# A batch-2 attention decode step with an MLP beside it: the linear layers turned round, the last transfers cut and ordered anew

## The chip, the core and the metric

The kernel runs on one core of a Trainium2 chip. A core has a matrix engine (TensorE, PE in the profile; its weight loads are PEld), a vector engine (DVE), a scalar engine (ACT), GpSimd (POOL), a sequencer that here only issues transfers (SP), and 16 DMA engines between HBM and the on-chip memory SBUF. TensorE writes to PSUM, which has banks of 512 fp32 values in each of 128 partitions. The metric is the time of one execution on the device in microseconds, a median over runs.

## The reference

With x of 2 rows by 1024 (batch 2, one token), cut to what matters:

```python
q = x @ wq                                   # 2 x 4096: 32 heads of 128
scores = einsum(q, k_cache) * Dh ** -0.5     # k_cache, v_cache: 2 x 32 x 16384 x 128, bf16
a = einsum(softmax(scores), v_cache).reshape(2, 1, 4096) @ wo
h = gelu(layernorm(x) @ w1)                  # then a shift along the sequence
x1 = x + shifted(h) @ w2
b = x1 + gelu(layernorm(x1) @ w3) @ w4       # w3: 1024 x 3584, w4: 3584 x 1024
return g * a + (1 - g) * b                   # g = sigmoid of (x * gate_w).sum()
```

With one token the shift leaves zeros. The two caches are 537 MB, the weights some 35 MB.

## The kernel before

**Units.** The attention is cut into NU = 32 units u, each a pair of heads (hp = u // 2) for one of the two batch rows b = u % 2. A unit has 8.4 MB of K and 8.4 MB of V, each loaded by one DMA of 128 partitions x 64 KB. Row s of the cache lies so that a partition holds 256 consecutive rows j.

**Memory.** One tile `mem` has five cells of 32 KB per partition. K of even units lies in cells 0 and 1, of odd units in cells 1 and 2; so two consecutive K loads share cell 1. V lies in cells 3 and 4 (V of unit 30 in cells 0 and 1). At the start wq lies in cells 3 and 4, w1 and w2 in cell 2; w3 follows in cells 3 and 4, and w4 after it in the same place.

**Main loop.** For n from 0 to 31: `score_first(n)` (K chunks transposed by DVE at L424, multiplied by PE at L430, first the half that shares a cell with the next K); `load_k(n+1)`; `score_second(n)`; the softmax in two steps, `softmax_a(n)` and `softmax_b(n)`; in between, for n of 2 and more, `pv(n-2)` (L502: probabilities as stationary operand, V streamed in 512 columns, into four column groups of the PSUM bank `oacc`), `load_v(n-1)`, and `pv_end(n-2)` (L515 copies the bank, four fp32 matmuls at L520 with the constant `sel8` add the four groups and transpose, L532 scales into `OT`). When both batch rows of a head pair are done, `wo_project(hp)` (L403) adds that pair's share of the output into two PSUM banks `arow`. Every fourth n, `load_wo` loads wo for four heads, 1 MB, into a single buffer.

**The linear layers.** q (L249) and the four layers of the MLP (L219, class `LinearT`) use the weight matrix as stationary operand in blocks of 128 x 128 and stream the two activation columns past it; the result comes out transposed, as the next step needs it. lin1, lin2 and lin3 run at n = 0, lin4 at n = 1. lin3's `load` stands behind q, lin4's behind lin3 and V of unit 0 behind lin4, since each takes the place of the one before.

**The end.** For n = 31, V of unit 30 is loaded first and V of unit 31 in nine pieces (`PIECES`, counted in rows j: seven of 32, two of 16; 32 rows are 1 MB). `pv_last` streams the first six pieces as in `pv`, and takes the rest with V as stationary operand (L547), one matmul for each j. Then L554 scales, `wo_project(15)` adds the last pair, DVE and ACT copy one output bank each, and SP stores both in one DMA. The last `load_wo` (n = 29, heads 28 to 31) is cut by partitions into five DMAs: `cuts = (0, 1, 3, 7, 16, P)`.

**What sets the order.** All DMAs are issued by SP in program order; each waits in SP's queue until its destination is free, and what stands behind it waits too. The framework derives the waits from the tiles' regions, and uses eight DMA semaphores in turn. Of one DMA, each of the 16 engines moves a fixed share of the partitions, and it takes its shares of successive DMAs one after another.

Of the kernel before, what the change touches and what calls it, by code (L numbers as in the profile page):

```python
# [23 lines left out]
def kernel(  # L24
# [15 lines left out]
    nc = tc.nc  # L40
# [35 lines left out]
    def misc_psum(shape, dtype=FP32):  # L76
        return mps.tile(shape, dtype, tag="misc", name="misc")
# [116 lines left out]
    for k in range(NP):  # L194
        t = const.tile([P, NJ // 4, 2, 4], BF16, name=f"pt{k}")
        nc.gpsimd.memset(t[:], 0.0)
        pts.append(t)

    class LinearT:

        def __init__(self, W, actT, name, cell, offset):
# [9 lines left out]
        def load(self):  # L211
            nc.sync.dma_start(out=self.dst, in_=self.src)

        def compute(self):
            wc = self.dst.rearrange("p (r n) -> p r n", n=self.N)
            ps = misc_psum([P, self.C, B])
            for c in range(self.C):
                for r in range(self.R):
                    nc.tensor.matmul(  # L219
                        ps[:, c, :],  # L220
                        lhsT=wc[:, r, :].rearrange("p (m c) -> p c m", c=self.C)[:, c, :],
                        rhs=self.actT[:, r, :],
                        start=(r == 0),
                        stop=(r == self.R - 1),
                    )
            nc.vector.tensor_copy(out=self.acc[:], in_=ps[:])

    xn1T = mlp.tile([P, KC, B], BF16)
# [15 lines left out]
    nc.vector.tensor_copy(out=xT[:], in_=xin[:].rearrange("p b r -> p r b"))  # L244

    qps = misc_psum([P, H, B])
    for h in range(H):
        for r in range(KC):
            nc.tensor.matmul(  # L249
                qps[:, h, :],  # L250
                lhsT=wq_t[:, r, h * Dh : (h + 1) * Dh],
                rhs=xT[:, r, :],
                start=(r == 0),
                stop=(r == KC - 1),
            )
    lin3.load()
    qT = const.tile([P, H, B], BF16)
# [79 lines left out]
    def gelu_T(pre, dst, C):  # L337
# [10 lines left out]
        )  # L348
        nc.vector.tensor_tensor(out=dst, in0=th[:], in1=pre, op=ALU.mult)

    def mlp_post1():
# [9 lines left out]
        layernorm_T(x1T[:], xn2T[:], "ln2")  # L361

    NH2 = D // 512
    arow = [rps.tile([B, 512], FP32, name=f"arow{k}") for k in range(NH2)]

    def mlp_post4():

        omg = mlp.tile([P, B], FP32, name="omg")
        nc.vector.tensor_scalar(
            out=omg[:], in0=g_rep[:], scalar1=-1.0, scalar2=1.0, op0=ALU.mult, op1=ALU.add  # L370
        )
        nc.vector.tensor_tensor(out=bT[:], in0=lin4.acc[:], in1=x1T[:], op=ALU.add)
        nc.vector.tensor_tensor(
            out=bT[:], in0=bT[:], in1=omg[:].unsqueeze(1).to_broadcast([P, KC, B]), op=ALU.mult
        )
        W = 512 // KC
        for k in range(NH2):
            for c in range(KC):
                nc.tensor.matmul(  # L379
                    arow[k][:].rearrange("b (m c) -> b c m", c=KC)[:, c, :],  # L380
                    lhsT=bT[:, c, :],
                    rhs=ident_f[:, k * W : (k + 1) * W],
                    start=(c == 0),
                    stop=False,
                    skip_group_check=True,
                )
# [3 lines left out]
    wo_view = A_wo.rearrange("(h d) n -> d h n", d=Dh)  # L390
    wo_tiles = {}

    def load_wo(q):
        t = wopool.tile([P, WOH, D], BF16, name="wo")
        cuts = (0, P) if q < H // WOH - 1 else (0, 1, 3, 7, 16, P)
        for a, z in zip(cuts, cuts[1:]):
            nc.sync.dma_start(out=t[a:z], in_=wo_view[a:z, q * WOH : (q + 1) * WOH, :])
        wo_tiles[q] = t

    def wo_project(hp):  # L400
        for k in range(NH2):
            for h in (2 * hp, 2 * hp + 1):
                nc.tensor.matmul(  # L403
                    arow[k][:],
                    lhsT=OT[:, h, :],
                    rhs=wo_tiles[h // WOH][:, h % WOH, k * 512 : (k + 1) * 512],
                    start=False,
                    stop=(h == H - 1),
                    skip_group_check=True,
                )  # L410

    S_tiles = {}
    st_tiles = {}
# [44 lines left out]
    def softmax_b(u):  # L458
        st, Dm = st_tiles.pop(u)
        R_ps = misc_psum([P, P])  # L460
        nc.tensor.matmul(R_ps[:], lhsT=ones_f[:], rhs=Dm[:], start=True, stop=True)  # L461
        nb = stat.tile([P, 1], FP32, name="nb")
        rs = stat.tile([P, 1], FP32, name="rs")
        Pt = pts[u % NP]
        halves = [slice(e * HALF, (e + 1) * HALF) for e in range(2)]
        for rows in halves:
            nc.vector.tensor_reduce(out=nb[rows], in_=R_ps[rows, rows], axis=AX.X, op=ALU.min)  # L467
        for e, rows in enumerate(halves):
            nc.scalar.activation(  # L469
                out=Pt[rows, :, e, :].rearrange("p (m a) k -> p a k m", a=GT // 4),  # L470
                in_=st[rows, :, 0:NG].rearrange("p (a k) m -> p a k m", k=4),
                func=ACTF.Exp,
                bias=nb[rows],
                scale=scale,
                accum_out=rs[rows],
            )
# [51 lines left out]
    def pv_end(u):  # L528
        hp, b = units[u]
        ot = misc_psum([P, 2])  # L530
        pv_sum(u, ot, True, True)
        nc.vector.tensor_scalar(  # L532
            out=OT[:, 2 * hp : 2 * hp + 2, b], in0=ot[:], scalar1=g_rep[:, b : b + 1],
            scalar2=None, op0=ALU.mult,
        )
        if b == B - 1:
            wo_project(hp)

    def pv_last(u):
        hp, b = units[u]  # L540
        ot = misc_psum([P, 2])
        moving = sum(PIECES[:6]) // 4
        pv_moving(u, 0, moving, moving)
        pv_sum(u, ot, False, False)
        V = v_view(u)
        for j in range(4 * moving, NJ):
            nc.tensor.matmul(  # L547
                ot[:],
                lhsT=V[:, j, :],
                rhs=pts[u % NP][:, j // 4, :, j % 4],  # L550
                start=False,
                stop=(j == NJ - 1),
            )
        nc.vector.tensor_tensor(  # L554
            out=OT[:, 2 * hp : 2 * hp + 2, b], in0=ot[:], in1=rinvs[u % NP][:], op=ALU.mult
        )
        wo_project(hp)

    for n in range(NU):
        score_first(n)  # L560
        if n == 0:
            compute_gate()
            layernorm_T(xT[:], xn1T[:], "ln1")
            lin1.compute()
            mlp_post1()
            lin2.compute()
            mlp_post2()
        if n + 1 < NU:
            load_k(n + 1)
        else:  # L570
            load_v(NU - 2)
        score_second(n)
        softmax_a(n)
        if n == 0:
            lin3.compute()
            gelu_T(lin3.acc[:], h2T[:], FC)
            load_wo(0)
            lin4.load()
        elif n == 1:
            lin4.compute()  # L580
# [12 lines left out]
    pv(NU - 2)  # L593
    pv_end(NU - 2)
    pv_last(NU - 1)

    out_row = mlp.tile([B, D], BF16)
    nc.vector.tensor_copy(out=out_row[:, 0:512], in_=arow[0][:])
    nc.scalar.activation(out=out_row[:, 512:1024], in_=arow[1][:], func=ACTF.Copy)
    nc.sync.dma_start(out=out.rearrange("b s d -> (b s) d"), in_=out_row[:])  # L600


# [28 lines left out]
```

## Time and profile before

| | |
|---|---|
| median of 3 runs | 1350.43 us (1346.7 to 1350.57) |
| the profiled execution | 1351.2 us, span 1349.2 |
| PE, DVE, ACT, POOL busy | 802.4, 643.0, 127.4, 15.3 us |
| read from HBM | 572.53 MB, 424 GB/s over the span |
| PE instructions of the linear layers | q 256 matmuls; lin1 and lin2 64 each, lin3 and lin4 224 each |
| the linear layers on PE | q from 22.91 to 33.2, lin3 from 75.26 for 14.30, lin4 from 115.95 for 13.57 us |

The page cuts the span into 40 equal slices of 33.7 us. A DMA line gives the busy share of the 16 engines, a GB/s line what they moved; the two differ where an engine is busy but slow. In rows of instruction groups the numbers are start and length in us, then the engine, the line of the kernel, and the tiles written and read. The chain of waits goes back from the last instruction, at each step to what released it.

### The profile page before, as it was taken

To read this page: it belongs to the slowest core of one execution; us is meant where nothing else is said; L and a number is where in the kernel's file an instruction comes from. 1 tells how busy PE (TensorE), PEld (TensorE's weight loads), DVE (VectorE), ACT (ScalarE), POOL (GpSimd) and SP (SyncE) were. 2 spreads that over 40 slices of the span, in tenths; PEclk is the share of its full clock that TensorE was granted. 3 is DMA by queue.
4 is the path that set the end of the run, shared out by engine and by line. 5 is a ranking of instruction groups with operands and counts; after the bars stand their busy time and mean duration, and the time that the engine had idled before them with its cause. 6 is when DMAs were issued, how large, how long until landed. Compare 5 with 4: busy or idle time off the path is not lost.

```text
span 1349.2 us, 12232 instructions
## 1 busy us (share of the span) xinstructions
PE 802.4 (59%) x5470; PEld 368.1 (27%) x5470; DVE 643.0 (48%) x501; ACT 127.4 (9%) x197; POOL 15.3 (1%) x54
## 2 busy tenths in 40 slices
PE   2679676554567645556664546666455666555464
PEld 2456222222222222222222222222222222222122
DVE  0444555543455554445555444555434455544250
ACT  0010100111111001111001111100111110011110
POOL 1000000000000000000000000000000000000000
PEclk9967887777888777778877778887667888777886
DMA  9999999999999999999999999999999999999996
GB/s 405 433 419 395 432 434 434 435 434 430 432 432 430 429 434 434 432 432 434 436 434 434 434 432 432 428 432 435 432 434 430 428 434 436 432 428 434 352 434 288
DMA packets 15803, 573.31 MB, mean 425 GB/s; under 512 B 1797, under 2 KB 1797, under 8 KB 6151
## 3 DMA queue, kind: packets, MB, share of 16 engines
q1 hardware_dynamic: 15751, 572.54, 99.0%
q8 instruction: 42, 0.69, 0.2%
q14 instruction: 10, 0.08, 0.0%
HBM read 572.53 MB, written 0.00 MB: 424 GB/s over the span
## 4 chain that ended last, share of the span: by engine, by line
DMA 67%; PE 17%; DVE 12%; issue 4%; ACT 0%; SPq 0%; POOL 0%; ACTq 0%; DVEq 0%
DMA mem<-in_A_k_cache_dram 65%; PE S L430 13%; DVE KT L424 12%; PE misc L219 3%; DMA mem<-in_A_v_cache_dram 2%; PE oacc L502 0%; PE arow L379 0%; ACT pt L469 0%; PE arow L403 0%; PE misc L547 0%; PE misc L520 0%; PE misc L461 0%; PE misc L480 0%; POOL ln_rstd L330 0%; DVE nb L467 0%
## 5 line engine op out<-in xcount | busy, mean ns | idle before, releaser
L430 PE MATMUL S<-KT,qw 128*128 128x512 bf16 x2048 | 553.1, 420 | 390.4 <-DVE KT L424 389.3
L424 DVE STREAM_TRANSPOSE KT<-mem 128x2048 f32<-128x2048 f32 x256 | 571.5, 2284 | 306.6 <-DMA mem<-in_A_k_cache_dram 247.6
L430 PEld LDWEIGHTS <-qw 128*128 128x128 bf16 x2048 | 220.2, 108 | 715.2 <-issue 540.6
L502 PE MATMUL oacc<-mem,pt 128*8 128x512 bf16 x2032 | 118.3, 384 | 16.0 <-DMA mem<-in_A_v_cache_dram 16.0
L455 ACT ACTIVATE Dm<-ident_s,m 128x128 f32<-128x128 f32 x32 | 12.9, 404 | 986.8 <-DVE m L453 986.8
L469 ACT ACTIVATE pt<-St,nb 64x256 bf16<-64x256 f32 x64 | 89.9, 1404 | 79.2 <-DVE nb L467 65.6
L532 DVE TENSOR_SCALAR OT<-misc,g_rep 128x2 bf16<-128x2 f32 x31 | 6.9, 222 | 144.9 <-PE misc L520 144.9
L502 PEld LDWEIGHTS <-pt 128*8 128x8 bf16 x2032 | 47.0, 87 | 83.6 <-issue 32.6
L480 PE MATMUL misc<-rs,lmat 128*128 128x1 f32 x62 | 17.7, 355 | 78.7 <-ACT pt L469 78.7
L482 DVE RECIPROCAL rinv<-misc 128x1 f32<-128x1 f32 x31 | 5.2, 169 | 102.2 <-PE misc L480 102.2
L451 DVE STREAM_TRANSPOSE St<-S 128x512 f32<-128x512 f32 x32 | 22.9, 717 | 63.8 <-PE S L430 63.8
L520 PE MATMUL misc<-sel,osb 128*128 128x2 f32 x256 | 34.5, 257 | 27.1 <-ACT osb L515 27.1
L520 PEld LDWEIGHTS misc<-sel,osb 128*128 128x128 f32 x256 | 31.8, 195 | 43.7 <-ACT osb L515 43.7
L480 PEld LDWEIGHTS misc<-rs,lmat 128*128 128x128 f32 x62 | 15.1, 302 | 91.4 <-ACT pt L469 91.2
L219 PEld LDWEIGHTS <-mem 128*128 128x128 bf16 x576 | 36.2, 169 | 1.7 <-issue 0.9
L469 ACT ACTIVATION_READ_ACCUMULATOR pt<-St,nb 64x1 f32 x64 | 30.6, 477 | 0.0
L515 ACT ACTIVATE osb<-oacc,rinv 128x512 f32<-128x512 f32 x31 | 21.4, 689 | 73.9 <-PE oacc L502 73.9
L249 PE MATMUL misc<-xT,mem 128*128 128x2 bf16 x256 | 7.1, 165 | 26.1 <-DVE xT L244 23.3
L281 POOL TENSOR_TENSOR qw<-qd,mask 128x16 bf16<-128x16 bf16 x32 | 8.4, 266 | 1165.1 <-PE S L430 1136.5
L403 PE MATMUL arow<-wo,OT 128*2 128x512 bf16 x64 | 20.1, 444 | 0.3 <-DVE OT L554 0.3
L467 DVE TENSOR_REDUCE nb<-misc 64x1 f32<-64x64 f32 x64 | 14.2, 222 | 5.0 <-PE misc L461 0.9
L461 PE MATMUL misc<-Dm,ones_f 128*128 128x128 f32 x64 | 15.6, 327 | 0.0
(83 smaller groups left out, 109.4 us busy)
## 6 DMA issues: line engine op xcount, KB each, us to landing
mem<-in_B_w_dram SPq DMA_DIRECT2D x2, 7168.0 KB, 29.1
wo<-in_A_wo_dram SPq DMA_DIRECT2D x7, 1024.0 KB, 31.8
mem<-in_A_v_cache_dram SPq DMA_DIRECT2D x7, 1024.0 KB, 30.0
mem<-in_B_w_dram SPq DMA_DIRECT2D x2, 2048.0 KB
mem<-in_A_v_cache_dram SPq DMA_DIRECT2D x2, 512.0 KB, 18.7
wo<-in_A_wo_dram SPq DMA_DIRECT2D x1, 896.0 KB, 35.9
mem<-in_A_k_cache_dram SPq DMA_DIRECT2D x32, 28.2
mem<-in_A_v_cache_dram SPq DMA_DIRECT2D x31, 33.3
```

The costliest lines, as they stand in the source:

```text
L219: nc.tensor.matmul(ps[:, c, :], lhsT=wc[:, r, :].rearrange("p (m c) -> p c m", c=self.C)[:, c, :], rhs=self.actT[:, r, :], start=(r == 0), ...
L403: nc.tensor.matmul(arow[k][:], lhsT=OT[:, h, :], rhs=wo_tiles[h // WOH][:, h % WOH, k * 512 : (k + 1) * 512], start=False, stop=(h == H - ...
L424: nc.vector.transpose(out=kt[:], in_=Kc.rearrange("p j d -> p (j d)").bitcast(FP32))
L430: nc.tensor.matmul(S, lhsT=t[:, v, NG - 1 - m : NG - 1 - m + P], rhs=ktb[:, half * GT : (half + 1) * GT, w, :, e], start=(first and n == 0 ...
L451: nc.vector.transpose(out=st[:].rearrange("p j r -> p (j r)"), in_=S[:])
L461: nc.tensor.matmul(R_ps[:], lhsT=ones_f[:], rhs=Dm[:], start=True, stop=True)
L467: nc.vector.tensor_reduce(out=nb[rows], in_=R_ps[rows, rows], axis=AX.X, op=ALU.min)
L469: nc.scalar.activation(out=Pt[rows, :, e, :].rearrange("p (m a) k -> p a k m", a=GT // 4), in_=st[rows, :, 0:NG].rearrange("p (a k) m -> p ...
L480: nc.tensor.matmul(tot_ps[:, 0:1], lhsT=lmat[:], rhs=rs[:], start=True, stop=True)
L502: nc.tensor.matmul(acc[QP * q : QP * q + 8, :], lhsT=pts[u % NP][:, g].rearrange("p h k -> p (h k)"), rhs=v_view(u)[:, 4 * g : 4 * g + 4, ...
L515: nc.scalar.activation(out=osb[:], in_=oacc[u % 2][:], func=ACTF.Copy, scale=rinvs[u % NP][:, 0:1] if scaled else 1.0,)
L520: nc.tensor.matmul(ot[:], lhsT=osb[:, k * Dh : (k + 1) * Dh], rhs=sel8[:, k : k + 5 : 4], start=(k == 0), stop=(last and k == 3),)
```

## The change

- **Linear layers.** `wide_bank` makes the activations (2 columns) the stationary operand and streams the weights in 512 columns past it. The K blocks r are dealt to four column groups of a PSUM bank (rows 0, 32, 64, 96), which `copy_bank` copies to SBUF, on ACT for even banks and on DVE for odd ones. Then one fp32 matmul for each 128 columns, with the copy as stationary operand and two columns of `sel8` as moving operand, adds the four groups and transposes. q does this for 8 banks, lin1, lin2 and lin4 for 2, lin3 for 7; lin3's copies go to cell 0 of `mem`. In the MLP layers the 128 columns of a select are taken with a stride of C (8 or 28) elements.
- **V of unit 31** comes in 11 pieces (six of 32, three of 16, two of 8 rows), and `pv_last` streams only the first three pieces; the other 160 rows j go through L547's form.
- **wo.** No load is cut by partitions any more. At n = 29 only heads 28 and 29 are loaded; heads 30 and 31 are loaded at n = 31, behind the pieces of V and behind `pv_end(29)` in the program.
- **The output banks.** `arow[1]` lies at partition 32 of its bank, `wo_project` alternates between the two banks, and each bank has its own copy and store, the second issued by ACT.
- **Small loads.** `load_probes`, at n = 29 after `pv_end(27)` and so between `load_v(28)` and `load_wo`, issues six DMAs of a few rows of `gate_w` into overlapping regions of a tile `probe` that nothing reads.

```diff
-    PIECES = [32] * 7 + [16] * 2
+    PIECES = [32] * 6 + [16] * 3 + [8] * 2
...
+    def copy_bank(j, dst, src):
+        if j % 2 == 0:
+            nc.scalar.activation(out=dst, in_=src, func=ACTF.Copy)
+        else:
+            nc.vector.tensor_copy(out=dst, in_=src)
+
+    def wide_bank(j, actT, weight, R, dst):
+
+        acc = oacc[j % 2]
+        for r in range(R):
+            q = r % Q4
+            nc.tensor.matmul(
+                acc[QP * q : QP * q + B, :],
+                lhsT=actT[:, r, :],
+                rhs=weight[:, r, :],
+                start=(r < Q4),
+                stop=(r >= R - Q4),
+            )
+        copy_bank(j, dst, acc[:])
...
-        def compute(self):
+        def compute(self, wide):
             wc = self.dst.rearrange("p (r n) -> p r n", n=self.N)
+            for j in range(self.N // 512):
+                at = slice(j * 512, (j + 1) * 512)
+                wide_bank(j, self.actT, wc[:, :, at], self.R, wide[:, at])
             ps = misc_psum([P, self.C, B])
             for c in range(self.C):
-                for r in range(self.R):
-                    nc.tensor.matmul(
-                        ps[:, c, :],
-                        lhsT=wc[:, r, :].rearrange("p (m c) -> p c m", c=self.C)[:, c, :],
-                        rhs=self.actT[:, r, :],
...
+                nc.tensor.matmul(
+                    ps[:, c, :],
+                    lhsT=wide.rearrange("p (m c) -> p c m", c=self.C)[:, c, :],
+                    rhs=sel8[:, 0:B],
...
-    for h in range(H):
-        for r in range(KC):
+    for j in range(H // HB):
+        qo = qwide[:, j % 2]
+        wide_bank(j, xT, wq_t[:, :, j * 512 : (j + 1) * 512], KC, qo)
+        for k in range(HB):
             nc.tensor.matmul(
...
-    arow = [rps.tile([B, 512], FP32, name=f"arow{k}") for k in range(NH2)]
+    arow_t = [rps.tile([QP * k + B, 512], FP32, name=f"arow{k}") for k in range(NH2)]
+    arow = [arow_t[k][QP * k : QP * k + B, :] for k in range(NH2)]
...
-    def load_wo(q):
+    def load_wo(h0, n):
         t = wopool.tile([P, WOH, D], BF16, name="wo")
-        cuts = (0, P) if q < H // WOH - 1 else (0, 1, 3, 7, 16, P)
-        for a, z in zip(cuts, cuts[1:]):
-            nc.sync.dma_start(out=t[a:z], in_=wo_view[a:z, q * WOH : (q + 1) * WOH, :])
-        wo_tiles[q] = t
+        nc.sync.dma_start(out=t[:, 0:n, :], in_=wo_view[:, h0 : h0 + n, :])
+        for k in range(n):
+            wo_tiles[h0 + k] = t[:, k, :]
...
+    probe = const.tile([17, 70], BF16, name="probe")
+
+    def load_probes():
+        for n, pitch, width in (
+            (17, 60, 20), (2, 512, 30), (4, 256, 40), (8, 128, 50), (11, 93, 60), (13, 78, 70),
+        ):
+            nc.sync.dma_start(
+                out=probe[0:n, 0:width],
+                in_=gate_w[0 : n * pitch].rearrange("(p f) -> p f", p=n)[:, 0:width],
+            )
...
-        moving = sum(PIECES[:6]) // 4
+        moving = sum(PIECES[:3]) // 4
...
+            if n == NU - 3:
+                load_probes()
+            if n == NU - 1:
+                load_wo(H - 2, 2)
         softmax_b(n)
         if n % 4 == 1 and n > 1:
-            load_wo(n // 4)
+            load_wo(n - 1, min(WOH, H - 2 - (n - 1)))
...
-    nc.sync.dma_start(out=out.rearrange("b s d -> (b s) d"), in_=out_row[:])
+    out_row = mlp.tile([QP + B, 512], BF16)
+    rows = out.rearrange("b s d -> (b s) d")
+    nc.vector.tensor_copy(out=out_row[0:B, :], in_=arow[0])
+    nc.sync.dma_start(out=rows[:, 0:512], in_=out_row[0:B, :])
+    nc.scalar.activation(out=out_row[QP : QP + B, :], in_=arow[1], func=ACTF.Copy)
+    nc.scalar.dma_start(out=rows[:, 512:1024], in_=out_row[QP : QP + B, :])
```

More of the change, by code (lines that the diff above doesn't have):

```diff
@@ L212, in load @@
             nc.sync.dma_start(out=self.dst, in_=self.src)
-        def compute(self):
+        def compute(self, wide):
             wc = self.dst.rearrange("p (r n) -> p r n", n=self.N)
+            for j in range(self.N // 512):
+                at = slice(j * 512, (j + 1) * 512)
+                wide_bank(j, self.actT, wc[:, :, at], self.R, wide[:, at])
             ps = misc_psum([P, self.C, B])
             for c in range(self.C):
-                for r in range(self.R):
-                    nc.tensor.matmul(
-                        ps[:, c, :],
-                        lhsT=wc[:, r, :].rearrange("p (m c) -> p c m", c=self.C)[:, c, :],
-                        rhs=self.actT[:, r, :],
-                        start=(r == 0),
-                        stop=(r == self.R - 1),
-                    )
+                nc.tensor.matmul(
+                    ps[:, c, :],
+                    lhsT=wide.rearrange("p (m c) -> p c m", c=self.C)[:, c, :],
+                    rhs=sel8[:, 0:B],
+                    start=True,
+                    stop=True,
+                )
             nc.vector.tensor_copy(out=self.acc[:], in_=ps[:])
@@ L246 @@
     qps = misc_psum([P, H, B])
-    for h in range(H):
-        for r in range(KC):
-            nc.tensor.matmul(
[L250 to L254, printed above, removed]
+    HB = 512 // Dh
+    qwide = mlp.tile([P, D], FP32, tag="wide", name="wide")[:].rearrange("p (t n) -> p t n", t=2)
+    for j in range(H // HB):
+        qo = qwide[:, j % 2]
+        wide_bank(j, xT, wq_t[:, :, j * 512 : (j + 1) * 512], KC, qo)
+        for k in range(HB):
+            nc.tensor.matmul(
+                qps[:, j * HB + k, :],
+                lhsT=qo[:, k * Dh : (k + 1) * Dh],
+                rhs=sel8[:, 0:B],
+                start=True,
+                stop=True,
             )
@@ L349, in gelu_T, with wide4 @@
         nc.vector.tensor_tensor(out=dst, in0=th[:], in1=pre, op=ALU.mult)
+    def wide4():
+        return mlp.tile([P, D], FP32, tag="wide", name="wide")[:]
     def mlp_post1():
@@ L379, in mlp_post4 @@
                 nc.tensor.matmul(
-                    arow[k][:].rearrange("b (m c) -> b c m", c=KC)[:, c, :],
+                    arow[k].rearrange("b (m c) -> b c m", c=KC)[:, c, :],
                     lhsT=bT[:, c, :],
@@ L391 @@
     wo_tiles = {}
-    def load_wo(q):
+    def load_wo(h0, n):
         t = wopool.tile([P, WOH, D], BF16, name="wo")
-        cuts = (0, P) if q < H // WOH - 1 else (0, 1, 3, 7, 16, P)
-        for a, z in zip(cuts, cuts[1:]):
-            nc.sync.dma_start(out=t[a:z], in_=wo_view[a:z, q * WOH : (q + 1) * WOH, :])
-        wo_tiles[q] = t
+        nc.sync.dma_start(out=t[:, 0:n, :], in_=wo_view[:, h0 : h0 + n, :])
+        for k in range(n):
+            wo_tiles[h0 + k] = t[:, k, :]
     def wo_project(hp):
-        for k in range(NH2):
-            for h in (2 * hp, 2 * hp + 1):
+        for h in (2 * hp, 2 * hp + 1):
+            for k in range(NH2):
                 nc.tensor.matmul(
-                    arow[k][:],
+                    arow[k],
                     lhsT=OT[:, h, :],
-                    rhs=wo_tiles[h // WOH][:, h % WOH, k * 512 : (k + 1) * 512],
+                    rhs=wo_tiles[h][:, k * 512 : (k + 1) * 512],
                     start=False,
@@ L410, in wo_project @@
                 )
+    probe = const.tile([17, 70], BF16, name="probe")
[6 more added lines that the diff above has]
+                in_=gate_w[0 : n * pitch].rearrange("(p f) -> p f", p=n)[:, 0:width],
+            )
     S_tiles = {}
@@ L563 @@
             layernorm_T(xT[:], xn1T[:], "ln1")
-            lin1.compute()
+            lin1.compute(wide4())
             mlp_post1()
-            lin2.compute()
+            lin2.compute(wide4())
             mlp_post2()
@@ L574 @@
         if n == 0:
-            lin3.compute()
+            lin3.compute(region(0, 2 * F).bitcast(FP32))
             gelu_T(lin3.acc[:], h2T[:], FC)
-            load_wo(0)
+            load_wo(0, WOH)
             lin4.load()
         elif n == 1:
-            lin4.compute()
+            lin4.compute(wide4())
             mlp_post4()
@@ L595 @@
     pv_last(NU - 1)
-    out_row = mlp.tile([B, D], BF16)
-    nc.vector.tensor_copy(out=out_row[:, 0:512], in_=arow[0][:])
-    nc.scalar.activation(out=out_row[:, 512:1024], in_=arow[1][:], func=ACTF.Copy)
-    nc.sync.dma_start(out=out.rearrange("b s d -> (b s) d"), in_=out_row[:])
+    out_row = mlp.tile([QP + B, 512], BF16)
[4 more added lines that the diff above has]
+    nc.scalar.dma_start(out=rows[:, 512:1024], in_=out_row[QP : QP + B, :])
 _INS = ['A_x', 'A_k_cache', 'A_v_cache', 'A_wq', 'A_wo', 'B_x', 'B_w1', 'B_w2', 'B_w3', 'B_w4', 'gate_w']
```

## The prediction

> **What bounds the kernel now.** I read the page's slices and queues first, then the chain of waits, then stretches of the span.
>
> ```profile
> DMA  9999999999999999999999999999999999999996
> GB/s 405 433 419 395 432 434 434 435 434 430 432 432 430 429 434 434 432 432 434 436 434 434 434 432 432 428 432 435 432 434 430 428 434 436 432 428 434 352 434 288
> q8 instruction: 42, 0.69, 0.2%
> DMA 67%; PE 17%; DVE 12%; issue 4%; ACT 0%; SPq 0%; POOL 0%; ACTq 0%; DVEq 0%
> ```
>
> All 16 DMA engines are busy throughout at about 434 GB/s, and 573 MB at that rate is 1321 us of the 1349.2. Computation matters only where it leaves a DMA engine without work, or after the last byte. The slices that fall short are the first ones, the fourth (395), slice 38 (352) and the last. Stretches around the two in the middle:
>
> ```profile
> 128.00:132.00 4.00, 3.15 (x38) 2.85 (x37) 0.88 (x5) 1.46 (x3) 0.00 (x0) 0.50 0.79 262
> 1232.00:1248.00 16.00, 8.05 (x29) 3.14 (x29) 10.06 (x5) 0.00 (x0) 0.00 (x0) 0.68 1.00 434
> 1248.00:1264.00 16.00, 12.12 (x101) 4.86 (x98) 8.86 (x6) 0.42 (x2) 0.00 (x0) 1.00 1.01 266
> 1264.00:1280.00 16.00, 1.87 (x12) 1.63 (x13) 0.84 (x4) 3.49 (x5) 0.00 (x0) 0.67 0.99 427
> ```
>
> The last two columns are DMA share and GB/s. At 128 the queue is dry (share 0.79): V(0) waits for w4's place, which lin4 holds. At 1248 the engines are busy (1.01) but move 266: the loss is 16 x (434-266)/434 = 6.2 us. What runs there is the last wo load, cut by rows into five DMAs (1, 2, 4, 9 and 112 partitions). The seven earlier wo loads, uncut, show nothing like it. The chain shows the price, and the tail:
>
> ```profile
> 1208.43 28.18 DMA mem<-in_A_k_cache_dram
> 1246.98 37.75 DMA mem<-in_A_k_cache_dram
> 1338.54 1.05 PE oacc L502 x8
> 1342.19 1.28 PE misc L547 x48
> 1343.50 0.60 PE misc L547 x16
> 1344.34 1.88 PE arow L403 x4
> 1346.24 0.59 ACT out_row L599
> ```
>
> Last I read the landings, which the trace records for each DMA once per DMA engine. An 8.4 MB K or V load takes each engine 19.36 us, 1 MB of wo 2.42 to 2.45. The engines drift apart: an instruction fetch (q8) sets one engine back about 1.45 us, and mostly the same nine are hit. So V(28), issued at 1222.73, should end at 1250.24 on the fastest engine (call it F) and, by 1236.61+19.36, at 1255.97 on the slowest. The slowest engine sets the end; its last piece lands at 1343.46.
>
> **The change part by part**, made against the profiled execution: span 1349.2, time 1351.2, which is 0.8 above the median of 1350.43.
>
> *Last wo load whole.* K(31) lands last at 1284.73. Undisturbed it would be 1236.61 + 19.36 (V28) + 2.42 (wo) + 19.36 = 1277.75. The cuts cost 6.98, and they go: **-7.0**.
>
> *Six probe loads (load_probes, at n=29 between V(28) and wo).* They write overlapping rows of one tile. SP waits for the landing of an earlier DMA whose bytes the next one overwrites, and for the DMA eight before (eight DMA semaphores):
>
> ```profile
> SPq L97 <- DMA mem<-in_A_k_cache_dram: 363.5, 28, 16.1
> SPq L108 <- DMA mem<-in_A_v_cache_dram: 23.9, 3, 13.0
> ```
>
> The first line is a K load waiting for the K load before it, where their regions share a cell. So each probe should wait for the one before, and behind the last stand wo and K(31) in SP's queue. The first is behind V(28) in its engine's ring. One step, issue to landing on an idle queue, is 1.24 us for the output store (1346.86 to 1348.10); V(0)'s first packet starts 0.95 after its issue, and with 0.35 to post the landing I take 1.45. Probes 1 to 3 pass on low-numbered engines, which are the fast ones (the cut pieces of 2 and 4 rows land early, bar one engine). The fourth uses eight engines and meets a slow one, so it lands at slowest + 0.2. Then probe 5 (1.45), probe 6's issue (0.1), wo's issue (0.45), first packet (0.95), half a wo (1.22): K(31) starts at slowest + 4.4, against + 1.2 without probes: **+3.2**. Below: 0 if nothing waits, and 1.7 if only the fifth probe meets a slow engine. Above: all five steps after the slowest engine, 3.2 + 3 x 1.45 = 7.6. The joint restart adds **+0.5**: V(0)'s first packets after the dry queue took 3.0 to 3.3 against 2.42. After it no engine is ahead or behind, and the fetches of the last 80 us put one of them 1.45 back, where the slowest engine now loses 0.6: **+0.85**.
> The Trainium skill, "DMA: Bandwidth & Descriptors", section "Anatomy of one DMA", fits a fixed 2.0 us per DMA, for loads issued by GpSimd. By it the step after the fourth probe would be dearer and the sum about 0.6 worse; the store's 1.24 speaks for less.
>
> *Wo of heads 30 and 31 after the V pieces.* Bytes are the same, **0** in transfer. SP issues it when the fourth piece has landed, some 10 us of queue before the end, so nothing runs dry.
>
> *The tail.* Now 1343.46 to 1349.18 is 5.72 after the last byte. In the new order the V sum is closed while wo's 1.22 us of transfer run: eight L547 (0.3), the scaling (0.25), hidden. If that cover were gone it would cost 0.6. After the last byte remain wo_project, whose two accumulators now sit in different column groups (1.88 becomes about 1.05; the 64 of L502 below show four groups overlapping), copy 0.7, store 1.24, closing 1.1, steps 0.1: 4.2. **-1.5** (0 if the groups do not overlap and ACT, which issues no DMA in this trace, needs 0.7 longer for its store than SP; -2 if PE is at full clock by then).
>
> *Linear layers.* The unit prices are three rows from n=29 and the old lin4:
>
> ```profile
> 1219.06 3.63 PE L502 MATMUL oacc<-mem,pt 128*8 128x512 bf16 x64
> 1222.80 0.69 ACT L515 ACTIVATE osb<-oacc,rinv 128x512 f32<-128x512 f32 x1 [1.87 <-PE oacc L502]
> 1223.54 1.05 PE L520 MATMUL misc<-sel,osb 128*128 128x2 f32 x8 [0.85 <-ACT osb L515]
> 115.95 13.57 PE L219 MATMUL misc<-h2T,mem 128*128 128x2 bf16 x224
> ```
>
> A 512-column matmul in a column group costs 57 ns (107 at half clock), a bank copy 0.69, an fp32 select two passes of 131 ns (232 at 1340, at clock 0.50). *q*: 64x57 + 64x131 = 12 us, at most 22 at half clock, against 10.4; K(0) lands at 43.76 and the q chain has 11 us to spare, so 0, with 1 us at risk. *lin1, lin2*: 0.9 + 2.1 against 4.0 each; K(1) needs only the wide part, 0. *lin3*: 14.3 becomes 3.2 + 1 (eight matmuls fill a bank in 0.46 and its copy takes 0.69, but ACT and DVE take turns) + 56 x 0.13 to 0.23 = 11.5 to 17; I take 15.4, nearer the slow end, as L219 runs at clock 0.50 there now. w4 can be issued after the wide part, near 81 where it was 89.58; the fast engines had run out at 90.36, 1.2 us dry, gone. *lin4*: V(0) waits for 56 wide matmuls (3.2 to 6) where it waited 13.57, so its issue moves from 129.56 to about 121, under the 126 that the queue needs; the 3.4 us dry (0 to 1.5 on engines already behind) go. Against this, K(2)'s issue (105.41, now needed by 105.4 for the fast engines and 107.6 for the slow) follows lin3's end, 1 to 3 us later. On the slowest engine I take **-2.0**, between -3.4 and +2. Fewer PE instructions mean some three fetches fewer of 42: 0, at best -1.5.
> The skill's "TensorEngine Tiling (Array Packing)", section "PSUM Bottleneck", says that tiling speeds the array but not the emptying of PSUM. By that rule alone, with one engine copying at the row's 0.69, lin3's seven banks would take an estimated 4.8 us and the sum would stay as it is, since w4's issue has more room than that.
>
> Sum: -7.0 + 3.2 + 0.5 + 0.85 - 1.5 - 2.0 = -5.95. From the median: 1350.4 - 5.95 = **1344.5**.
>
> **Rivals.**
> *Probes cost nothing* (SP does not wait for overlapping rows): 3.2 + 0.5 + 0.85 come back, 1340. The waits for K speak against it. 0.12.
> *The slowdown comes from any DMA on a few engines, not from the 112 shifted rows*: V(28) loses 3.7 to 4.2 again, and the gain is 2: 1348.5, no change. For it: V(28) itself was slow beside the small pieces. Against: probes carry some 40 to 140 bytes a row. 0.25, with a late lin3 in it.
> *Slower: lin3's strided fp32 selects.* L219 costs 62 ns a weight load where L249, unstrided, costs 27. If fp32 suffers likewise, 56 x 0.4 = 22 us put lin3's end 12 later, K(2)'s issue at 117 and every engine dry for 10: +10 + 2 - 6 = +6, 1356. It decides once a pass costs over about 0.3 us (end 8 later, gain gone). Against it: L520's contiguous fp32 load already takes 192 ns where L249's bf16 takes 104, so the stride may have nothing left to slow. 0.13.
>
> **How the numbers follow.** Forecast 0.5 (1342 to 1347), free probes 0.12, no change 0.25, slower 0.13. About 0.3%, 4 us, is what a measurement of this kernel can tell from no change. Faster takes nine tenths of the forecast and all of the free probes, 0.57; within 0.3%, 0.29; slower 0.14, with a little from the no-change case. The range cuts the far half of the slower case and the far end of the free probes: 1338.5 to 1353.
>
> **What would show it.** Right: near 1250 to 1264 no stretch that is busy at 266 GB/s; six short SP issues each ended by the landing before, and K(31) issued some 3 us after V(28)'s last landing; all engines within 2 us afterwards; V(0) issued before 126; under 4.5 us from the last landing to the end. Wrong: K(2) issued after 110, S matmuls of n=0 later than 48, lin3's selects over 0.3 us a pass, or probes issued back to back.

## The result, and the profile after

The changed kernel takes 1359.4 us (median of 4 runs, 1357.39 to 1360.63); the kernel before, run beside it, 1350.5 (1346.7 to 1351.18). The ratio is 1.007, with a 95% interval from 1.0047 to 1.0094: slower by some 9 us where 6 us less were forecast. The profiled execution of the changed kernel took 1360.63 us, its span is 1358.0.

The slices and queues of its page, in the lines that answer to those of before:

```profile
DMA  9987999999999999999999999999999999999996
GB/s 402 433 360 315 431 433 433 431 431 427 433 433 432 424 438 433 435 435 426 436 433 433 431 429 433 431 431 428 433 431 429 433 427 432 435 435 435 425 424 277
q8 instruction: 39, 0.64, 0.2%
DMA 67%; PE 17%; DVE 12%; issue 3%; ACT 0%; SPq 0%; POOL 0%; DVEq 0%; ACTq 0%
```

The 352 in slice 38 is gone (425 now). But the third and fourth slices, 68 to 136 us, fell from 419 and 395 to 360 and 315, and there the engines are not slow, they have nothing to do (8 and 7 tenths). Stretches of the changed kernel (us, busy time of PE, its weight loads, DVE, ACT and POOL, then granted clock, DMA share, GB/s):

```profile
112.00:122.00 10.00, 7.86 (x26) 2.95 (x26) 8.53 (x5) 0.00 (x0) 0.00 (x0) 0.72 0.01 6
123.00:127.00 4.00, 3.42 (x16) 1.40 (x15) 4.00 (x3) 0.00 (x0) 0.00 (x0) 1.00 0.83 344
1262.00:1278.00 16.00, 13.20 (x110) 5.83 (x107) 9.29 (x9) 1.57 (x3) 0.00 (x0) 1.00 1.00 423
1328.00:1333.00 5.00, 3.22 (x36) 1.13 (x39) 0.00 (x0) 0.00 (x0) 0.00 (x0) 0.53 0.74 290
```

From 112 to 122 hardly a packet starts (share 0.01): w4 has landed on all 16 engines by 114.6, and nothing stands behind it until K(2). At 1262, where the last wo load now passes, the full rate stands (423, it was 266). At 1328 there is a new gap. SP's issues around the first gap, in the kernel before and in the changed one (start, length):

```profile
64.69 0.33 SPq L97 DMA_DIRECT2D mem<-in_A_k_cache_dram  x1
89.58 0.33 SPq L212 DMA_DIRECT2D mem<-in_B_w_dram  x1
105.41 0.33 SPq L97 DMA_DIRECT2D mem<-in_A_k_cache_dram  x1
129.56 0.33 SPq L100 DMA_DIRECT2D mem<-in_A_v_cache_dram  x1
```
```profile
71.72 0.33 SPq L97 DMA_DIRECT2D mem<-in_A_k_cache_dram  x1
92.71 0.33 SPq L232 DMA_DIRECT2D mem<-in_B_w_dram  x1
121.69 0.33 SPq L97 DMA_DIRECT2D mem<-in_A_k_cache_dram  x1
135.50 0.33 SPq L100 DMA_DIRECT2D mem<-in_A_v_cache_dram  x1
```

These are K(1), w4, K(2) and V(0). K(2) goes out 16.3 us later. The chain of waits of the changed kernel says what stood in front of it:

```profile
46.29 1.88 PE misc L275 x8
51.86 0.72 POOL ln_rstd L356
52.78 2.23 DVE KT L464
55.06 5.84 PE S L470 x16
93.36 12.86 PE misc L241 x56
...
1307.50 20.63 DMA probe<-in_gate_w_dram
1328.15 4.24 DMA probe<-in_gate_w_dram
1340.98 12.88 DMA wo<-in_A_wo_dram
1353.90 1.06 PE arow L432 x4
1354.96 0.67 DVE out_row L643
```

q's last selects (L275), the layernorm behind them and the first K transposes are on the chain, where K(0)'s landing had been the releaser; then lin3's selects (L241). At the end the chain goes through the probes, and after the last wo landing (1353.90) only 4.1 us are left.

The 8.8 us of span, read on the slowest DMA engine from its landings (us):

| | before | after | difference |
|---|---|---|---|
| V(28) last, undisturbed (1236.61 + 19.36 before) | 1255.97 | 1270.2 | +14.2 |
| from there to K(31) last | 28.8 | 20.7 | -8.1 |
| from there to the last byte | 58.7 | 63.0 | +4.3 |
| last byte to end of span | 5.72 | 4.10 | -1.6 |

Of the second row, 1.2 is half of a wo load that now comes later, and lies in the third. So the uncut wo load gave -7, the probes cost some 3, the tail gave 1.6, and the beginning lost 14.

### The profile page after: what moved, and what is told of

It reads as the page before. It is cut to its first block, busy times and chain, and to the rows that moved or that the text cites. A ratio compares the mean times of both kernels' runs of the same rounds, so it can differ in the third digit from the quotient of the medians.

```text
span 1358.0 us, 11505 instructions
## 1 busy us (share of the span) xinstructions
PE 806.9 (59%) x5086; PEld 366.8 (27%) x5086; DVE 650.4 (48%) x511; ACT 133.5 (10%) x208; POOL 15.2 (1%) x54
## 4 chain that ended last, share of the span: by engine, by line
DMA 67%; PE 17%; DVE 12%; issue 3%; ACT 0%; SPq 0%; POOL 0%; DVEq 0%; ACTq 0%
DMA mem<-in_A_k_cache_dram 57%; PE S L470 12%; DVE KT L464 11%; DMA probe<-in_gate_w_dram 7%; PE misc L241 2%; DMA xin<-in_A_x_dram 2%; PE oacc L210 1%; PE misc L275 1%; DMA wo<-in_A_wo_dram 1%; DMA mem<-in_A_v_cache_dram 0%; PE oacc L542 0%; PE arow L409 0%; ACT pt L509 0%; ACT mem L201 0%; DVE wide L203 0%
## 5 line engine op out<-in xcount | busy, mean ns | idle before, releaser
L542 PE MATMUL oacc<-mem,pt 128*8 128x512 bf16 x2008 | 115.5, 382 | 8.6 <-DMA mem<-in_A_v_cache_dram 8.6
L560 PE MATMUL misc<-sel,osb 128*128 128x2 f32 x256 | 34.5, 257 | 26.7 <-ACT osb L555 26.7
L210 PE MATMUL oacc<-mem,xT 128*2 128x512 bf16 x64 | 9.4, 612 | 24.0 <-DVE xT L266 23.2
L507 DVE TENSOR_REDUCE nb<-misc 64x1 f32<-64x64 f32 x64 | 14.2, 222 | 5.0 <-PE misc L501 0.9
L275 PEld LDWEIGHTS misc<-sel,wide 128*128 128x128 f32 x64 | 14.2, 328 | 7.4 <-issue 4.4
L203 DVE COPY wide<-oacc 128x512 f32<-128x512 f32 x7 | 4.8, 691 | 22.9 <-PE oacc L210 22.9
```

The lines of the kernel that those rows point to most:

```text
L210: nc.tensor.matmul(acc[QP * q : QP * q + B, :], lhsT=actT[:, r, :], rhs=weight[:, r, :], start=(r < Q4), stop=(r >= R - Q4),)
L275: nc.tensor.matmul(qps[:, j * HB + k, :], lhsT=qo[:, k * Dh : (k + 1) * Dh], rhs=sel8[:, 0:B], start=True, stop=True,)
L542: nc.tensor.matmul(acc[QP * q : QP * q + 8, :], lhsT=pts[u % NP][:, g].rearrange("p h k -> p (h k)"), rhs=v_view(u)[:, 4 * g : 4 * g + 4, ...
L560: nc.tensor.matmul(ot[:], lhsT=osb[:, k * Dh : (k + 1) * Dh], rhs=sel8[:, k : k + 5 : 4], start=(k == 0), stop=(last and k == 3),)
```

## The experiments

Each ratio is to runs of the kernel before made together with the experiment's own: their median is 1350.38 us for e1 to e4, 1350.32 for e5 to e8 and 1349.91 for e9 to e12. Two theories for the 14 us: the new linear layers are slower, in q and lin1 to lin3, because of their fp32 selects; or the probes and the new end cost more than thought. Two for the -7: the 112 shifted rows of the last piece were slow, or any DMA on a few engines is.

**e1_linear_old**: the changed kernel with q and all MLP layers in their old form.

```diff
-            lin3.compute(region(0, 2 * F).bitcast(FP32))
+            lin3.compute()
... (lin1, lin2, lin4 and q's loop likewise)
```

> The changed kernel with q and all four MLP layers in the old form (weights stationary); everything else as changed. Theory A (the fp32 selects, at 0.22 to 0.23 us a pass, make q 15 us and lin3 4 us longer, K(2) is issued at 121.7 and all DMA engines run dry for 10 us): K(2) issued at 105 to 106, first landing of V(0) back from 162.2 to about 150.8, time 1359.4 - 11 = 1348, still with the 3.4 us dry before V(0). Theory B (the probes' waits in SP's queue cost the time): 1356 or more, since the probes stay.

Measured: 1344.75 us, 0.9961 of before [0.995, 0.9973]. V(0) is issued at 129.3 (129.6 before) and V(28) lands last at 1257.0, 13 us earlier than in the changed kernel and 1 later than before (undisturbed). So 13 of the 14 us lie in the linear layers, and all the rest of the change is worth -5.6, which is the sum of the table's other parts (-7 + 3 - 1.6).

**e2_q_old**: the changed kernel with q's old loop alone.

```diff
-    for j in range(H // HB):
-        wide_bank(j, xT, ...)
+    for h in range(H):
+        for r in range(KC):
```

> The changed kernel with only q in the old form. Theory A: S of n=0 starts at 46 and not at 55, everything up to K(2) moves 9 us earlier, K(2) issued near 113, dry only 1 to 2 us: 1359.4 - 9 = 1350.5. Theory B: unchanged, 1358 to 1360. If lin3 and not q is what counts: a gain of 4 at most, 1355.

Measured: 1348.67 us, 0.9985 [0.9976, 0.9993]. S of n=0 starts at 46.09 as before, K(2) is issued at 112.6: 9.1 earlier than in the changed kernel, still 7.2 later than before. So q carries about 9 us and lin1 to lin3 about 7. (The 7 is against the profiled run of before, which had the later of the two starts told at the end; e2 had the earlier one, and against e4, which had it too, K(2) is 10 later: 112.6 for 102.4.)

**e5_selects_bf16**: the changed kernel with the bank copies and the select's two columns in bf16.

```diff
+    sel8b = const.tile([P, 8], BF16)
+    nc.vector.tensor_copy(out=sel8b[:], in_=sel8[:])
...
-                    rhs=sel8[:, 0:B],
+                    rhs=sel8b[:, 0:B],
...
-        return mlp.tile([P, D], FP32, tag="wide", name="wide")[:]
+        return mlp.tile([P, D], BF16, tag="wide", name="wide")[:]
...
-            lin3.compute(region(0, 2 * F).bitcast(FP32))
+            lin3.compute(region(0, F))
```

> The changed kernel with the bank copies and sel8 in bf16, so that each select is one pass with a bf16 stationary operand; wide matmuls, copies, probes, order as changed. (The partial sums are rounded to bf16.) Theory A1 (the two fp32 passes of 0.22 us make the linear layers long): a select falls from 0.45 us to 0.06 or less, q ends near 35 and not 48, lin3 near 84, K(2) issued before 106, no dry queue at 113 to 123: 1359.4 - 14 = 1345, or 1342 if V(0)'s old 3.4 us wait is gone too. Theory A2 (the wide matmuls with their bank copies, which wait for each other in two banks, make them long): q still ends after 43, K(2) after 115, time 1355 or more.

Measured: 1342.38 us, 0.9944 [0.9932, 0.9957], 17 us less than the changed kernel. q ends at 34.5, K(2) is issued at 100.45 and V(0) at 114.27; neither leaves the queue dry. Selects and an issue in its timeline, then the same selects of the changed kernel:

```profile
34.21 0.25 PE L277 MATMUL misc<-sel8b,wide 128*128 128x2 bf16 x4 [0.82 <-DVE wide L205]
76.50 1.94 PE L243 MATMUL misc<-sel8b,mem 128*128 128x2 bf16 x28 [0.71 <-ACT mem L203]
100.45 0.33 SPq L97 DMA_DIRECT2D mem<-in_A_k_cache_dram  x1
```
```profile
46.29 1.86 PE L275 MATMUL misc<-sel,wide 128*128 128x2 f32 x8 [0.82 <-DVE wide L203]
93.36 12.86 PE L241 MATMUL misc<-sel,mem 128*128 128x2 f32 x56 [0.70 <-ACT mem L201]
```

The same sums take 1.94 where they took 12.86 us: fp32 takes two passes a select (56 for 28), and each is over three times as long. The bank copies, which e5 writes in bf16 too, take 0.60 us on ACT and 0.69 on DVE in both kernels, so they are not the gain. That the selects' precision is the cause of the loss is shown; the column groups themselves are not a cause, as they are the same in both.

**e6_lin4_wide_only**: q and lin1 to lin3 old, lin4 new.

```diff
-            lin3.compute(region(0, 2 * F).bitcast(FP32))
+            lin3.compute_old()
... (q, lin1, lin2 likewise; lin4.compute(wide4()) stays)
```

> The changed kernel with q, lin1, lin2 and lin3 in the old form and only lin4 in the new one. Theory: lin4's wide part frees w4's place some 10 us after its start's old time, V(0) issued near 120 and not 129.3, the queue does not run dry there: against the version with all layers old (1344.75) the fast DMA engines gain 3.4 us and the slowest 0 to 2: 1343 to 1344.5. Rival (lin4's fp32 selects push K(3) and all that follows): 1346 or more.

Measured: 1342.54 us, 0.9948 [0.9936, 0.996]. lin4's wide matmuls take 3.19 us and V(0) goes out at 115.77, long before K(2) has passed. This part of the change does what it says, fp32 selects and all, as no transfer waits for those. And e5 is no faster than e6 (1342.38, 1342.54): in the other layers the new form won nothing here. Without the probes it does win a little, as e9 and e10 show below.

**e4_before_whole_wo**: the kernel before, with its last wo load whole.

```diff
-        cuts = (0, P) if q < H // WOH - 1 else (0, 1, 3, 7, 16, P)
+        cuts = (0, P)
```

> The kernel before with the last wo load in one DMA instead of five, nothing else. Theory: the 16 us at 266 GB/s go and K(31) lands last 7.0 us earlier, time 1350.5 - 7 = 1343.5, at about 434 GB/s from 1248 to 1264. Rival (the slowdown belongs to that place in the run or to the DMA engines' drift, not to the cuts): 1349 to 1350.5, the stretch still under 350 GB/s.

Measured: 1344.59 us, 0.9954 [0.9942, 0.9966], -5.8 by the medians where -7 was expected. K(31) lands last at 1275.9, 21.8 us after V(28); before it was 1284.7, and 28.8 after V(28) undisturbed. So 6.9 us are gained there, but from K(31) to the last byte e4 takes 60.0 us for 58.7, and 1.3 of them are lost again.

**e7_before_cut16** and **e12_before_cut64**: the kernel before, with the last wo load in rows 0 to 15 and 16 to 127, and in two halves of 64 rows.

```diff
-        cuts = (0, P) if q < H // WOH - 1 else (0, 1, 3, 7, 16, P)
+        cuts = (0, P) if q < H // WOH - 1 else (0, 16, P)
```

> The kernel before with the last wo load in two DMAs, rows 0 to 15 and rows 16 to 127: both run on all 16 engines (1 and 7 rows each), but the rows of an engine are shifted against those of K and V. Theory S (the shift of the 112 rows makes engines meet in the same rows of SBUF): 266 to 300 GB/s from 1248 to 1264 again, 1350. Theory F (loads on only 1, 2, 4 or 9 engines do it): as with the whole load, 1344.6, above 420 GB/s.

> The kernel before with the last wo load in two halves of 64 rows, each on all 16 engines with 4 rows per engine. Theory S (what counts is that an engine writes rows of SBUF which at that time another engine, ahead of or behind it, also fills): slow again, under 330 GB/s from 1248 to 1264 and 1348 to 1351. Rival (an odd row offset or 7 rows per engine did it): 1344.6, above 420 GB/s.

Measured: 1349.93, 0.9998 [0.9989, 1.0007], and 1350.02, 0.9998 [0.9988, 1.0007]. Neither cut uses fewer than 16 engines, and both are as slow as five pieces.

**e8_before_whole_plus_few**: the kernel before, its last wo load whole, and ahead of it four loads of 1, 2, 4 and 9 rows into a tile that nothing reads.

```diff
+            for a, z in ((0, 1), (1, 3), (3, 7), (7, 16)):
+                nc.sync.dma_start(out=few[a:z], in_=wo_view[a:z, q * WOH : (q + 1) * WOH, 0 : D // 2])
```

> The kernel before with the last wo load whole, and ahead of it four small loads with the rows of the old cuts (1, 2, 4 and 9 rows of four heads, half as long, into a tile of their own that nothing reads): few engines, but no shifted 112 rows. Theory S: 1344.6 as with the whole load. Theory F: the 7 us are back, 1350, under 350 GB/s from 1248 to 1264.

Measured: 1345.75, 0.997 [0.9958, 0.9982], near e4. Small loads on few engines cost little. The stretch that was busy at 266 GB/s before, in e4, e7, e8 and e12 in this order:

```profile
1248.00:1264.00 16.00, 11.98 (x105) 5.35 (x102) 7.78 (x8) 3.04 (x5) 0.00 (x0) 1.00 1.01 427
```
```profile
1248.00:1264.00 16.00, 12.05 (x93) 4.64 (x91) 6.80 (x5) 1.09 (x2) 0.00 (x0) 0.89 1.00 279
```
```profile
1248.00:1264.00 16.00, 13.96 (x113) 6.22 (x111) 9.68 (x7) 1.09 (x2) 0.00 (x0) 1.00 1.08 452
```
```profile
1248.00:1264.00 16.00, 11.72 (x103) 5.37 (x101) 7.03 (x6) 1.09 (x2) 0.00 (x0) 1.00 0.99 284
```

Where the rows of a load are dealt to the engines otherwise than those of the K and V loads around it, all engines are busy and move two thirds of the usual rate. The few-engine rival falls, at least for loads as small as those of e8. Why such a load is slow, no run shows.

**Without probes**: e3 is the changed kernel, e9 is e5, e10 is e6 and e11 is e1, each without the call.

```diff
-            if n == NU - 3:
-                load_probes()
```

> The changed kernel without the six probe loads. Theory A: only the gap in the V pieces at 1329 to 1333 goes, where SP waited for probes 4 and 5: 3 to 4 us, 1355.7. Theory B: 8 us or more, 1351 or less. If the pieces would wait for semaphores anyway: no change, 1359.

> The changed kernel with bf16 selects and without the probe loads (the partial sums are rounded to bf16). The two findings should add: 1342.4 - 3 = 1339.4, the last V pieces 1.24 to 2.5 us apart without a gap, 16 engines ending up to 6 us apart again. If the probes' pause only hides what the engines' drift then costs: no gain, 1342.

> Only lin4 in the new form (with fp32 selects), no probe loads, the rest as changed. 1342.5 - 3 = 1339.5, as with bf16 selects everywhere, since both keep the queue full up to V(0) and nothing after it differs. If the shorter q and lin3 of the bf16 selects are worth something by themselves, this one is slower than that by 1 or more.

> All linear layers old, no probe loads; left of the change are the whole wo loads, the V pieces with wo of two heads behind them, the two output banks and stores. From the version with probes (1344.75) less 3: 1341.8. From the kernel before with the whole wo load (1344.6) less the 1.5 us of the tail: 1343.1. Within 1341.5 to 1343.3 both hold. If the tail's gain were an artefact of the probes' pause: 1344.6.

| | with probes | without | ratio of the latter to before |
|---|---|---|---|
| changed kernel, e3 | 1359.4 | 1356.45 | 1.0044 [1.0032, 1.0056] |
| bf16 selects, e9 | 1342.38 | 1340.84 | 0.9931 [0.9918, 0.9943] |
| lin4 alone, e10 | 1342.54 | 1342.42 | 0.9942 [0.993, 0.9954] |
| linear layers old, e11 | 1344.75 | 1345.69 | 0.9962 [0.995, 0.9974] |

The medians differ by 3.0, 1.5, 0.1 and -0.9. Of the expected times only that of e3 was met: e9 came between its two (1339.4 and 1342), e10 was 3 us over 1339.5, e11 2 over the upper end of 1343.3. The last two are probably blurred by the two starts told below: the profiled runs of e10 and e11 had the later one, that of e6 the earlier one, and the single times of e6 and e11 fall in two groups (1342.3 to 1342.5 and 1343.9 to 1344.0; 1342.5 and 1344.7 to 1345.9). The rival named for e11, a tail gained only through the probes' pause, falls: its tail is 4.20. And e9 is faster than e10, 1340.70 to 1341.01 for 1342.02 to 1342.71: it issues K(2) at 100.52 (e10: 105.18), and V(0) lands last at 148.22 (149.76). So bf16 selects in the other layers, for which e10's expectation allowed 1 us or more, are worth 1.5 us against the later start; against e6, with the earlier one, they won nothing.

On the slowest engine, from V(28)'s last landing to the last byte, the kernels with probes (e1, e2, e5, e6, the changed one) take 82.5 to 83.7 us, those without 80.6 to 82.2: means 83.2 and 81.1. So the probes cost about 2 us. Where they cost it, SP's issues and waits of the changed kernel show:

```profile
1260.74 0.33 SPq L97 DMA_DIRECT2D mem<-in_A_k_cache_dram  x1
1264.30 0.25 SPq L447 DMA_DIRECT2D probe<-in_gate_w_dram  x1
...
1328.15 0.31 SPq L447 DMA_DIRECT2D probe<-in_gate_w_dram  x1
1328.52 0.33 SPq L108 DMA_DIRECT2D mem<-in_A_v_cache_dram  x1
1332.41 0.33 SPq L447 DMA_DIRECT2D probe<-in_gate_w_dram  x1
```
```profile
SPq L97 <- DVE KT L464: 351.8, 31, 28.5
SPq L447 <- DMA probe<-in_gate_w_dram: 36.3, 5, 14.6
```

They wait for each other, five times, 36.3 us in all. But SP's order is not the order of the source, as "What sets the order" above has it: wo is issued at 1238.49, right behind the first probe, and K(31), V(29), V(30) and the first piece of V(31) stand between the others, so these waits pass beside 8 MB transfers. Only probes 5 and 6 stand before short ones, the second and third piece of V(31), and the queue runs low: share 0.74 from 1328 to 1333, where e3 has

```profile
1328.00:1333.00 5.00, 3.24 (x36) 1.15 (x39) 0.00 (x0) 0.00 (x0) 0.00 (x0) 0.52 0.99 415
```

Of the 2.9 us between the two kernels 2.75 lie in these pieces, between the last landings of the second and the eleventh. After that pause the engines are nearly level: from the third piece on each lands on all of them within 0.3 to 1.9 us, against 6.4 to 6.5 in e3.

**The best version** is e9: bf16 selects, no probes, all else of the change. 1340.84 us (1340.7 to 1341.01) is 0.9931 of before and 18.6 us under the changed kernel, at the price of partial sums rounded to bf16.

## Why the prediction was wrong

**The step that failed is the linear layers**: -2.0, between -3.4 and +2, was forecast; K(2)'s issue moved 16.3 us (from 105.41 to 121.69, forecast "1 to 3 us later") and V(28)'s last landing 14. Two of its terms were wrong: the price of an fp32 select, 131 ns a pass, which holds at full clock and for contiguous operands only, and q's "11 us to spare". The 16.3 come from three stages.

*q, "12 us, at most 22, ... 11 us to spare, so 0, with 1 us at risk": +8.9.* Both halves were wrong. q took 24.9 us (23.17 to 48.1). The fp32 passes start 213 ns apart, where 131 was taken, and a 512-column matmul took 117 (1.88 us for 16), not 57; the first line is from q, the second from e6's lin4:

```profile
23.17 1.88 PE L210 MATMUL oacc<-mem,xT 128*2 128x512 bf16 x16 [23.17 <-DVE xT L266]
```
```profile
112.53 3.19 PE L210 MATMUL oacc<-mem,h2T 128*2 128x512 bf16 x56
```

These are the prices of half clock, as at 1340 before, where the passes start 213 apart too at a recorded clock of 0.50. The stretches print a granted clock of 1.00 in q, but the records of the clock only begin at 59.57 in this trace: before that, 1.00 means that nothing was recorded. In e5 they begin at 31.13, within q, and right behind that eight of the same matmuls take 0.60 us and not 1.02. A stretch and eight matmuls of the changed kernel, then eight of e5:

```profile
30.00:34.00 4.00, 4.00 (x28) 2.15 (x20) 0.69 (x1) 0.60 (x1) 0.00 (x0) 1.00 0.61 262
39.38 1.02 PE L210 MATMUL oacc<-mem,xT 128*2 128x512 bf16 x8
```
```profile
31.45 0.60 PE L212 MATMUL oacc<-mem,xT 128*2 128x512 bf16 x8
```

So a part of what e5 gains in q is the earlier full clock. In the changed kernel 64 x 0.213 + 64 x 0.107 = 20.5, with the prediction's own 107 ns for a matmul at half clock, is near its upper end of 22; the rest of the 24.9 is idle time between banks. And 11 us to spare was K(0)'s landing less the end of q, but layernorm stands between q and the first transposes in DVE's order. In the kernel before its last step and the transposes were

```profile
37.73 0.18 DVE L333 TENSOR_TENSOR xn1T<-ln_cen,ln_rstd 128x16 bf16<-128x16 f32 x1 [0.75 <-POOL ln_rstd L330]
43.78 4.50 DVE L424 STREAM_TRANSPOSE KT<-mem 128x2048 f32<-128x2048 f32 x2 [5.88 <-DMA mem<-in_A_k_cache_dram]
```

so the spare was 5.88. q ended 14.9 later (48.1 for 33.2), and 14.9 - 5.9 = 9.0 is what S of n=0 was late (55.06 for 46.15). By the chosen 12 us nothing would have been late; by the upper end of 22 some 5.7, not 1.

*lin1 and lin2, "0.9 + 2.1 against 4.0": +3.3*, from S to lin3's input xn2T. Their 16 passes took 3.97 and 3.76 us, not 2.1.

*lin3, 15.4: +4.1* from xn2T to K(2)'s issue. It took 18.8 (87.46 to 106.22), 12.86 of it selects, the slow end of the forecast, and 5.9 the wide part, forecast at 4.2: a pair of banks came every 1.30 us (L210 starting at 89.46, 90.76 and 92.06), since each waits for a copy; the first pair took 2.0, as both its copies stood behind work of the softmax. On this the Trainium skill's "TensorEngine Tiling (Array Packing)", section "PSUM Bottleneck", was the nearer: emptying PSUM is what tiling leaves slow, and the estimate from it was 4.8.

*lin4* did what was forecast: 3.2 us, and the dry stretch at V(0) is gone (V(0) is issued at 135.5, before K(2) has landed). The sign "V(0) before 126" failed only because K(2) was late; in e6 it is 115.77.

The slower rival, "lin3's strided fp32 selects" (1356, chance 0.13), had the place, K(2)'s issue and the dry queue behind it, and nearly the time, but the wrong size of its mechanism: a pass took 0.23, not over 0.3, and lin3 alone would have cost 4. The stride does something, as the weight loads of q (contiguous), lin3 (stride 28) and before's pv_end (contiguous) show, min/median/max in ns:

```profile
L275 PEld LDWEIGHTS misc<-sel,wide x64: 285/333/338, 26.4 to 47.7; 128*128 128x128 f32 x64
L241 PEld LDWEIGHTS misc<-sel,mem x56: 302/322/323, 93.4 to 105.8; 128*128 128x128 f32 x56
```
```profile
L520 PEld LDWEIGHTS misc<-sel,osb x256: 186/192/333, 161.3 to 1341.8; 128*128 128x128 f32 x128
```

Contiguous loads start 111 ns apart at full clock and 213 at half; lin3's strided ones 227 apart, alike where the records give 0.89 (94 to 98) and 0.50 (98 to 106), and those of lin1, lin2 and lin4 (stride 8) 238. So in these runs a strided fp32 load costs twice a contiguous one at full clock, and at half clock next to nothing more. The prediction took 131 in all of them but lin3: q ran at half clock, and lin1 and lin2 paid for the stride.

**The last wo load whole, -7.0**: right, and for the reason given. K(31) comes 6.9 earlier after V(28), e4 gains 5.8 as a whole, and e7, e12 and e8 show that it is the cutting by partitions and not the few engines. The Trainium skill's "DMA: Bandwidth & Descriptors", section "Rules for kernel authors", says that two transfers to disjoint halves of the partitions serialize, and advises one transfer of 128 partitions. The runs here agree with the advice, and e12 shows more than a serial order, a loss of about 5.4 us against the whole load of e4 (1350.02 for 1344.59).

**Probes, +3.2 + 0.5 + 0.85**: the wait was right, its place and size were not. K(31) is issued at 1260.74, before V(28) has landed everywhere (1270.2), and there is no joint restart: K(31)'s landings are 7.2 us apart, where "within 2 us" was the sign. The price was 2 to 3 us, at the pieces of V. The step that failed is the reading of the source's order as SP's.

**Wo of heads 30 and 31 at the end, 0; fewer fetches, 0**: nothing speaks against them. SP issues that wo load at 1340.98, when the fourth piece has landed (1340.92), as forecast; there are 39 instruction fetches for 42.

**The tail, -1.5**: right, 4.10 for 5.72. All kernels with the new end have 4.1 to 4.2, all with the old one 5.5 to 5.7. The four matmuls of the last wo_project take 1.01 us, forecast 1.05.

```profile
1353.90 1.01 PE L432 MATMUL arow<-wo,OT 128*2 128x512 bf16 x4 [0.92 <-DMA wo<-in_A_wo_dram]
```

Left open: V(0) lands 11.4 us later than before and V(28) 14.2. Of the 3 us between them 1.5 have come by K(30) (last landing 1249.56 for 1236.61), and 1.3 lie in V(28) itself, which lands 20.66 us after K(30) where 19.36 was taken for before. e2 and e3 show 20.6 there, e1 and e5 19.4; the cause is not known.

## What to carry to other kernels

Where transfers bound a kernel, cost a layer's new form by what its last instruction releases, and measure the spare to the next step in that engine's own order, not to the end of the layer. A price from the steady state does not hold for the first 50 us, and a contiguous fp32 stationary operand's does not hold for a strided one; a two-column sum is best given a bf16 stationary operand if the rounding is allowed. Do not cut one load of a stream by partitions otherwise than its neighbours: here it cost 5 to 7 us.

## What the hardware showed beside

- **A slow start of TensorE that the clock row does not print.** In the kernel before, matmuls of S start 427 ns apart until 50.8 us and 217 apart from there, and the first clock record begins at 50.87. In nine kernels with the old q the first record begins where the fast pace does, between 49.3 and 51.6.
- **Two starts.** Kernels with the old q have K(1) issued near 62.5 or near 65, and of those with all layers old V(0)'s first landing lies at 147.6 to 147.8 or at 150.6 to 151.3. It goes with the first full-clock stretch, which lasts 13.7 us (e4, e6, e7, e12; 10.2 in e2) or 3.4 (before, e1, e8, e10, e11). The kernel before and e4, from 54 to 58 us:

```profile
54.00:58.00 4.00, 4.00 (x25) 1.94 (x25) 0.44 (x1) 0.00 (x0) 0.00 (x0) 0.57 1.06 459
```
```profile
54.00:58.00 4.00, 4.00 (x36) 2.52 (x36) 2.14 (x2) 0.00 (x0) 0.00 (x0) 1.00 1.04 449
```

  It fits the spread of single times (before 1346.7 to 1351.18), and e9, in which the queue stays full early on (mean DMA share 1.00 from 58 to 146 us, 0.97 before), spreads over 0.3 us. What decides between the two was not found.
- **The price of a bf16 weight load with a stride**: 62 to 64 ns apart in e5's lin3, mostly 25 to 28 in its q, where it is contiguous.
